# Attention and two MoE layers on one core: the second group's q loads move to ScalarE's queue, the third pair's v cast to GpSimd, and half of the x casts to ScalarE

## The chip, the cores and the metric

The kernel runs on one core of a Trainium2 chip. The core has a matrix engine (TensorE, PE in the profile; its weight loads are the row PEld), VectorE (DVE), ScalarE (ACT), GpSimd (POOL) and SyncE (SP), which only issues transfers here. The metric is device time in microseconds for one launch, the median of several runs.

## The reference, cut to what matters

```python
# attention: q, k, v are (2, 12, 448, 64), cap = 30
scores = q @ k.T / sqrt(64)
scores = cap * tanh(scores / cap)
attn = exp(scores) / sum(exp(scores))
x = (attn @ v), heads side by side: 896 tokens x 768
# first MoE layer: 768 -> 2048 -> 768
h = x @ w_in1
x = where(h > 0, h, exp(min(h, 0)) - 1) @ w_out1
# second MoE layer: 768 -> 2048 -> 768
h = maximum(x @ w_in2, 0)
out = (h * h) @ w_out2
```

The weights arrive as 64-bit floats. The kernel computes in pairs of 32-bit parts: each operand is split into a high part, rounded to the type that TensorE multiplies, and a low part, the rest; a product is high by high, high by low and low by high.

## The kernel before

**Tiling.** The 24 heads are taken as 12 pairs of heads, n = 0 to 11; two pairs (four heads) form a group, whose q, k and v are loaded together. A head's 448 rows are three full chunks of 128 and a tail of 64. The tails of k and q have their own tiles, `kz` and `qz`, those of v the tile `vs`.

**One pair** passes through these steps. `turn(n)` transposes its k and q chunks on TensorE into the PSUM tile `pt`. `high(n)` copies `pt` to the high part `kqh` on ScalarE and `low(n)` makes the low part `kql` on VectorE. `scores(n, c)` for c = 0 to 3 multiplies k by q into a PSUM tile `sc`, of which there are two, so each waits until the `tanh` two before it has read its tile. `tanh(n, c)` and `exp(n, i)` run on ScalarE and write the tile `e`. `split_p(n, i)` splits `e` into `ph` and `pl` on VectorE (i = 0 are the first four blocks, i = 1 the rest; both tiles exist once). `prep_v(n)` splits v into `vh` (cast) and `vl` (subtraction). `pv(n, i)` multiplies on TensorE into `po`. `pv_out(n)` copies `po` to `pvs` on ScalarE and moves the sums of exp to `den`. `norm(n)` takes their reciprocal `rd` on VectorE and sends it through DRAM (`far`, `bc`). `norm_x(n)` multiplies (`xn`) and splits the result into `xh` and `xl`, the operands of the first MoE layer.

**Order.** The whole program is written out by hand: every engine runs its instructions in the order of the code. The loop over n works on several pairs at once: in round n ScalarE and VectorE handle the scores of pair n, TensorE the products of pair n-1 and the transposes of pair n+2, and VectorE the normalisation of pair n-3. TensorE's order in a round is scores(n, 2), pv(n-1, 1), scores(n, 3), turn(n+2), scores(n+1, 0) and (n+1, 1), pv(n, 0). In round 0 nine idle products (18 matmul rows) stand where pv(n-1, 1) would be, and turn(2) comes behind scores(1, 1).

**Queues.** Nearly all transfers are issued on SP's queue, one after the other; at the start group 0's first q, `cap` and one piece of weights are on ScalarE's queue. Group 1 (pairs 2 and 3) is loaded while pair 0 is worked on. Each of SP's and ScalarE's transfers raises one of eight semaphores (DMAHW0 to DMAHW7), which are handed out in turn over both queues, and a transfer is issued only when the transfer before it on its semaphore has landed.

**Behind the loop** the MoE layers run on TensorE (`mm_in`, `moe1_out`, `moe2_out`), with the weights split piece by piece on VectorE and ScalarE while TensorE multiplies.

Of the kernel before, what the change touches and what calls it, by code (L numbers as in the profile page):

```python
# [26 lines left out]
def attention_moe_kernel(  # L27
# [12 lines left out]
    nc = tc.nc  # L40
    B, H, S, D = q.shape
# [46 lines left out]
    qzs = [one.tile([P, 4, D], F32, name=f"qz{i}") for i in range(2)]  # L88
# [4 lines left out]
    def fill_kq(i, eng):  # L93
        eng.memset(kzs[i], 0.0)
        eng.memset(qzs[i][D:], 0.0)
# [4 lines left out]
        if i < 2:  # L100
            eng.memset(vss[i][:, :, D:], 1.0)

    def load_group(g, what="kqvw", pp=None, dma=nc.sync.dma_start):

        if 2 * g >= len(pairs):
            return
        b, hp = pairs[2 * g]
        h0, nh = (0, 4) if pp is None else (2 * pp, 2)
        hs = slice(2 * hp + h0, 2 * hp + h0 + nh)
        if g not in nat:  # L110
            nat[g] = {x: lp.tile([P, NFULL, 4, D], F32, name=x, tag=x) for x in "kqv"}
        tail = slice(NFULL * P, S)
        for x, src in (("k", k), ("q", q)):
            if x in what:
                t = nat[g][x][:, :, h0:h0 + nh]
                src = src[b, hs]
                for c in range(NFULL):
                    dma(  # L118
                        t[:, c], src[:, c * P:(c + 1) * P].rearrange("h p d -> p h d")
                    )  # L120
                if x == "q":
                    dma(
                        qzs[g % 2][:D, h0:h0 + nh], src[:, tail].rearrange("h p d -> p h d")
                    )
                else:
                    for hh, r in enumerate(ROWS):
                        dma(
                            kzs[g % 2][r, h0 // 2:(h0 + nh) // 2, r],
                            src[hh::2, tail].rearrange("h p d -> p h d"),
                        )  # L130
        if "v" in what:
            for c in range(NFULL):
                dma(
                    nat[g]["v"][:, c, h0:h0 + nh],
                    v[b, hs, c * P:(c + 1) * P].rearrange("h p d -> p h d"),
                )
        if "w" in what:
            for hh, r in enumerate(ROWS):
                dma(
                    vss[g % 2][r, h0 // 2:(h0 + nh) // 2, :D],  # L140
                    v[b, hs][hh::2, tail].rearrange("h p d -> p h d"),
                )

    def prep_v(n):
        if n >= len(pairs):
            return
        g, pp = divmod(n, 2)
        vh, vl = vhs[n % 3], vls[n % 3]
        vn = nat[g]["v"][:, :, 2 * pp:2 * pp + 2]
        h, l = (t.rearrange("p (c h) d -> p c h d", h=2)[:, :, :, :D] for t in (vh, vl))  # L150


        (nc.vector if n > 1 else nc.gpsimd).tensor_copy(h, vn)
        nc.gpsimd.tensor_tensor(l, vn, h.bitcast(F32), op=ALU.subtract)


# [2 lines left out]
    def turn_one(to, n, u, c):  # L159
        g, pp = divmod(n, 2)  # L160
        hs = slice(2 * pp, 2 * pp + 2)
        if c < NFULL:
            src = nat[g]["kq"[u]][:, c, hs].rearrange("p h d -> p (h d)")
        elif u == 0:
            src = kzs[g % 2][:, pp]
        else:
            src = qzs[g % 2][:, hs].rearrange("p h d -> p (h d)")
        nc.tensor.transpose(to, src, ident)  # L168
# [25 lines left out]
    def idle_products(to, n):  # L194
        for _ in range(n):
            nc.tensor.matmul(to[:, 0, :P], ident, ident, start=True, stop=True)

    def first_pair():

        idle = psc.tile([P, 2, W], F32, name="sc", tag="sc")
        warm = lambda n: idle_products(idle, n)
        qk = [ap_.tile([P, 2, W], F32R, name=x, tag=x) for x in ("kqh", "kql")]
        st["qk", 0] = qk
        warm(8)
        pieces = []
        for u, cs, pool, tag, after in (
            (0, range(NFULL), ps1, "pt", 2),
            (1, range(NFULL + 1), ps1, "po", 0),  # L210
            (0, range(NFULL, NFULL + 1), psc, "sc", 6),
        ):
            t = pool.tile([P, 2, W], F32, name=tag, tag=tag)
            at = slice(cs[0] * P, (cs[-1] + 1) * P)
            for c in cs:
                turn_one(t[:, u, c * P:(c + 1) * P], 0, u, c)
            warm(after)
            pieces.append((t[:, u, at], *(x[:, u, at] for x in qk)))
        for t, h, l in pieces:
            nc.scalar.copy(h, t)  # L220
        for t, h, l in pieces:
            nc.vector.tensor_tensor(l, t, h.bitcast(F32), op=ALU.subtract)
# [27 lines left out]
    def exp(n, i):  # L250
        e = st["e", n][:, PARTS[i]]
        nc.scalar.activation(e, e, AF.Exp, scale=capt)  # L252

    def split_p(n, i, copy=nc.vector.tensor_copy):
        if n < 0:
            return
        if i == 0:
            st["p", n] = [
                ap_.tile([P, NB - 1, S], F32R, name=x, tag=x, bufs=1) for x in ("ph", "pl")
            ]  # L260
        blocks = slice(PARTS[i].start, min(PARTS[i].stop, NB - 1))
        e, h, l = (t[:, blocks] for t in [st["e", n]] + st["p", n])
        copy(h, e)
        nc.vector.tensor_tensor(l, e, h.bitcast(F32), op=ALU.subtract)
# [52 lines left out]
    def norm_x(n, copy=nc.vector.tensor_copy):  # L317

        if n < 0:
            return []  # L320
        b, hp = pairs[n]
        xn = ap_.tile([P, S], F32, name="xn", tag="xn")
        hi, lo = xh[:, hp, b * S:(b + 1) * S], xl[:, hp, b * S:(b + 1) * S]

        def x():
            for u, r in enumerate(ROWS):
                nc.vector.tensor_tensor(  # L327
                    xn[r], st["pvs", n][:D, u], st["bc", n][:, u], op=ALU.mult
                )

        return [
            x,
            lambda: copy(hi, xn),  # L333
            lambda: nc.vector.tensor_tensor(lo, xn, hi.bitcast(F32), op=ALU.subtract),  # L334
        ]
# [154 lines left out]
    def emit(steps):  # L490
        for step in steps:
            step()
# [42 lines left out]
    with tc.manual_schedule():  # L535
        fill_kq(0, nc.vector)
        load_group(0, "k", 0)
        load_group(0, "q", 0, dma=nc.scalar.dma_start)
        nc.scalar.dma_start(capt, cap.unsqueeze(0).to_broadcast([P, 1]))
        ws.load(nc.scalar.dma_start)  # L540
        load_group(0, "kq", 1)
        load_group(0, "vw", 0)
        fill_kq(1, nc.gpsimd)
        load_group(1, "kq")
        load_group(0, "vw", 1)
        ws.load()
        load_group(1, "vw")
# [2 lines left out]
        fill_v(2, nc.gpsimd)  # L550
        np_ = len(pairs)
        first_pair()
        nc.vector.reciprocal(tsc, capt)
        nc.vector.tensor_scalar(tsc, tsc, 1.0 / math.sqrt(D), None, op0=ALU.mult)
        prep_v(0)
# [18 lines left out]
        for n in range(np_):  # L574
            last = n == np_ - 1
            tanh(n, 0)
            if n:
                high(n + 1)
            tanh(n, 1)
            if not n:  # L580
                high(n + 1)
            split_p(n - 1, 1)
            prep_v(n + 1)
            exp(n, 0)
            low(n + 1)
            if n == 2:
                emit(second[3:])
            scores(n, 2)
            pv(n - 1, 1)
            scores(n, 3)  # L590
            if n:
                turn(n + 2)
            else:
                idle_products(ps1.tile([P, 2, W], F32, name="po", tag="po"), 9)
            norm(n - 2)
            if last:
                emit(ws.start())
            tanh(n, 2)
            pv_out(n - 1)
            if 2 <= n < 7:  # L600
                ws.load()
            tanh(n, 3)
            exp(n, 1)
            emit(norm_x(n - 3))
            split_p(n, 0)
            if n == 1:
                second = ws.whole()
                emit(second[:3])
            scores(n + 1, 0)
            scores(n + 1, 1)  # L610
            if not n:
                turn(2)
            if last:

                begun.append(new_acc())
                mm_in(0, 0, begun[0], xh, xl, kb[0:6:2])
            pv(n, 0)

            if n % 2:
                load_group((n + 3) // 2, "qv" if n > 1 else "v")  # L620
            else:
                load_group(n // 2 + 2, "k" if n else "kq")
                load_group(n // 2 + 1, "w" if n else "")


# [12 lines left out]
        x, x_high, x_low = norm_x(np_ - 2)  # L638
# [9 lines left out]
        x, x_high, x_low = norm_x(np_ - 1, nc.scalar.copy)  # L648
# [166 lines left out]
```

## Time and profile before

| | |
|---|---|
| median of 3 runs | 595.95 us (595.73 to 596.18) |
| the profiled execution | 594.1 us, span 592.3 us |
| PE busy in the span | 583.4 us (98%) |
| PEld, DVE, ACT, POOL busy | 89%, 72%, 56%, 5% |
| granted TensorE clock, mean | 0.997 |

The span runs from the first instruction to the last one of the profiled execution; 1.8 us of its time lie around it. Times within the span are given as us from its start. A row of the timeline gives start, duration, engine, line of the kernel, operation, tiles, count and, in brackets, the engine's idle time before it with what ended it.

### The profile page before, as it was taken

The page shows a single profiled execution, that of the slowest core. Times are in us where ns is not written, and L with a number is a line of the kernel's source. Part 1 is how long each engine was busy: PE and PEld are TensorE (multiplying, and loading weights), DVE is VectorE, ACT ScalarE, POOL GpSimd, SP SyncE. Part 2 cuts the span into 40 slices and gives each one's busy share as a digit, 9 for nine tenths or more (in the row PEclk, how much of TensorE's full clock was granted, in tenths as well). Part 3 has the DMA queues.
Part 4 walks back from the last instruction along what each step waited for, and adds up shares of the span by engine and source line. Part 5 has one row for each costly group of instructions (what it writes and reads, how often), then busy time and mean ns, then how long its engine had stood idle before and what let it go on. Part 6 is the DMA issues. An engine that isn't in the chain of part 4 may idle for free.

```text
span 592.3 us, 8596 instructions
## 1 busy us (share of the span) xinstructions
PE 583.4 (98%) x3062; PEld 528.0 (89%) x3062; DVE 425.0 (72%) x845; ACT 334.2 (56%) x484; POOL 32.1 (5%) x46
## 2 busy tenths in 40 slices
PE   8899999999999999999999999999999999999997
PEld 8677777788999999999999999999999999999997
DVE  4599999989999888665666657777777599981000
ACT  5699999827898777433333335666666645441000
POOL 3110110000000000000000000000000011230000
PEclk9899999999999999999999999999999999999999
DMA  5645651024444333233333344333333346622000
GB/s 128 158 103 140 161 148 42 33 75 144 135 133 134 106 98 100 76 128 106 116 98 107 111 132 132 107 107 107 108 114 113 108 136 184 184 70 106 24 23 37
DMA packets 81980, 64.76 MB, mean 109 GB/s; under 512 B 38416, under 2 KB 77072, under 8 KB 81936
## 3 DMA queue, kind: packets, MB, share of 16 engines
q1 hardware_dynamic: 80432, 63.58, 36.8%
q10 hardware_dynamic: 1504, 0.62, 0.4%
q8 instruction: 24, 0.39, 0.3%
q14 instruction: 20, 0.16, 0.1%
HBM read 61.34 MB, written 2.80 MB: 108 GB/s over the span
## 4 chain that ended last, share of the span: by engine, by line
PE 90%; DMA 3%; DVE 3%; SPq 2%; ACT 1%; issue 1%; POOL 0%; ACTq 0%; POOLq 0%; DVEq 0%
PE acc L522 19%; PE acc L523 19%; PE acc L521 19%; PE po L287 8%; PE acc L746 7%; PE acc L745 7%; PE acc L747 7%; PE sc L235 4%; PE pt L168 1%; DMA q<-in_q_dram 1%; SPq L118 1%; DVE xn L327 1%; DMA far<-rd 1%; DMA bc<-far 1%; DMA qz<-in_q_dram 0%
## 5 line engine op out<-in xcount | busy, mean ns | idle before, releaser
L521 PE MATMUL acc<-xh,wh 128*128 128x448 f32 x384 | 139.8, 364 | 1.2 <-ACT xh L333 1.2
L522 PE MATMUL acc<-xl,wh 128*128 128x448 f32 x384 | 140.0, 365 | 0.2 <-DVE xl L334 0.2
L523 PE MATMUL acc<-xh,wl 128*128 128x448 f32 x384 | 139.9, 364 | 0.0
L446 ACT CAST wh<-wf 128x384 fp32r<-128x384 f32 (+2 forms) x114 | 57.9, 508 | 107.2 <-PE acc L522 87.5
L391 ACT ACTIVATE wf<-wst 128x384 f32<-128x384 f32 (+2 forms) x130 | 70.5, 543 | 60.5 <-DVE wl L441 33.7
L441 DVE TENSOR_TENSOR wl<-wf,wh 128x384 fp32r<-128x384 f32 (+2 forms) x116 | 63.6, 548 | 55.9 <-ACT wh L446 55.8
L521 PEld LDWEIGHTS acc<-xh,wh 128*128 128x128 f32 x384 | 72.1, 188 | 7.1 <-ACT xh L333 1.5
L522 PEld LDWEIGHTS acc<-xl,wh 128*128 128x128 f32 x384 | 72.1, 188 | 5.9 <-DVE xl L334 0.5
L523 PEld LDWEIGHTS acc<-xh,wl 128*128 128x128 f32 x384 | 72.1, 188 | 5.7 <-DVE wl L441 0.3
L432 DVE SCALAR_TENSOR_TENSOR wf<-wst,wf 128x384 uint32<-128x384 uint32 (+3 forms) x132 | 71.1, 539 | 0.1
L425 DVE SCALAR_TENSOR_TENSOR wf<-wst,wf 128x384 uint32<-128x384 uint32 (+3 forms) x132 | 70.9, 537 | 0.0
L522 PE MATMUL acc<-gl,wh 128*128 128x448 f32 x192 | 70.0, 365 | 0.0
L523 PE MATMUL acc<-gh,wl 128*128 128x448 f32 x192 | 70.0, 364 | 0.0
L521 PE MATMUL acc<-gh,wh 128*128 128x448 f32 x192 | 69.8, 364 | 0.0
L404 DVE TENSOR_SCALAR wf<-wf 128x384 uint32<-128x384 uint32 (+3 forms) x132 | 54.4, 412 | 0.7
L400 DVE TENSOR_SCALAR wf<-wf 128x384 f32<-128x384 f32 (+3 forms) x132 | 45.7, 346 | 7.5 <-ACT wf L391 7.5
L244 ACT ACTIVATE e<-sc,tsc 128x896 f32<-128x896 f32 (+1 forms) x48 | 43.4, 911 | 2.9 <-PE sc L235 2.9
L732 DVE COPY o<-acc 128x432 f32<-128x432 f32 (+1 forms) x8 | 4.5, 557 | 53.8 <-PE acc L747 45.7
L746 PE MATMUL acc<-wl,gh 128*128 128x432 f32 x112 | 40.3, 359 | 0.0
L745 PE MATMUL acc<-wh,gh 128*128 128x432 f32 x112 | 40.0, 357 | 0.0
L747 PE MATMUL acc<-wh,gl 128*128 128x432 f32 x112 | 39.9, 356 | 0.0
L252 ACT ACTIVATE e<-e,capt 128x1792 f32<-128x1792 f32 (+1 forms) x24 | 38.6, 1609 | 0.8
(94 smaller groups left out, 933.0 us busy)
## 6 DMA issues: line engine op xcount, KB each, us to landing
wst<-in_moe_w_in_dram SPq DMA_DIRECT2D x63, 384.0 KB, 3.2
wst<-in_moe_w_out_dram SPq DMA_DIRECT2D x24, 384.0 KB, 3.2
wst<-in_moe_w_out_dram SPq DMA_DIRECT2D x16, 432.0 KB, 3.2
wst<-in_moe_w_out_dram SPq DMA_DIRECT2D x16, 336.0 KB, 2.9
wst<-in_moe_w_out_dram SPq DMA_DIRECT2D x12, 256.0 KB, 2.7
bc<-far SPq DMA_DIRECT2D x12, 224.0 KB, 3.3
k<-in_k_dram SPq DMA_DIRECT2D x15, 128.0 KB, 3.7
q<-in_q_dram SPq DMA_DIRECT2D x15, 128.0 KB, 2.9
```

Of the source, the lines that this page charges most:

```text
L391: nc.scalar.activation(self.f[i], hi.bitcast(F32), AF.Abs)
L404: v.tensor_scalar(fb, fb, 3, 0x3FFFFFFF, op0=ALU.logical_shift_left, op1=ALU.bitwise_and)
L425: v.scalar_tensor_tensor(out=fb, in0=hi, scalar=0xC0000000, in1=fb, op0=ALU.bitwise_and, op1=ALU.bitwise_or,)
L432: v.scalar_tensor_tensor(out=fb, in0=lo, scalar=29, in1=fb, op0=ALU.logical_shift_right, op1=ALU.bitwise_or,)
L441: (v if dst is None else nc.gpsimd).tensor_tensor(wl, self.f[i], wh.bitcast(F32), op=ALU.subtract)
L446: (v.tensor_copy if self.alone else nc.scalar.copy)(wh, self.f[i])
L521: nc.tensor.matmul(acc, w[0], x[0], start=first, stop=False)
L522: nc.tensor.matmul(acc, w[0], x[1], start=False, stop=False)
L523: nc.tensor.matmul(acc, w[1], x[0], start=False, stop=last)
L745: nc.tensor.matmul(acc, gh[:, f, gs], w[0], start=a, stop=False)
L746: nc.tensor.matmul(acc, gh[:, f, gs], w[1], start=False, stop=False)
L747: nc.tensor.matmul(acc, gl[:, f, gs], w[0], start=False, stop=z)
```

## The change

Four edits. (1) `load_group` gets a letter "z" for the tail of q, which was part of "q". Group 1's three q chunks are no longer issued on SP's queue between its k and its q tail, but on ScalarE's queue, at the place in the code behind `first_pair()`; the tail stays on SP's queue. (2) The cast of `vh` for pair 2 moves from VectorE to GpSimd. (3) In odd rounds (3, 5, 7, 9 and 11, pairs 0, 2, 4, 6 and 8) the cast of `xh` moves from VectorE to ScalarE, behind exp(n, 1). (4) In these rounds `xl` on VectorE moves behind split_p(n, 0).

```diff
-    def load_group(g, what="kqvw", pp=None, dma=nc.sync.dma_start):
+    def load_group(g, what="kqzvw", pp=None, dma=nc.sync.dma_start):
...
-                if x == "q":
-                    dma(
-                        qzs[g % 2][:D, h0:h0 + nh], src[:, tail].rearrange("h p d -> p h d")
-                    )
-                else:
+                if x == "k":
                     for hh, r in enumerate(ROWS):
...
+        if "z" in what:
+            dma(qzs[g % 2][:D, h0:h0 + nh], q[b, hs, tail].rearrange("h p d -> p h d"))
...
-        (nc.vector if n > 1 else nc.gpsimd).tensor_copy(h, vn)
+        (nc.vector if n > 2 else nc.gpsimd).tensor_copy(h, vn)
...
-        load_group(1, "kq")
+        load_group(1, "kz")
         load_group(0, "vw", 1)
         ws.load()
         load_group(1, "vw")
...
         first_pair()
+        load_group(1, "q", dma=nc.scalar.dma_start)
         nc.vector.reciprocal(tsc, capt)
...
-            emit(norm_x(n - 3))
-            split_p(n, 0)
+            if n % 2:
+
+                steps = norm_x(n - 3, nc.scalar.copy)
+                emit(steps[:1])
+                split_p(n, 0)
+                emit(steps[1:])
+            else:
+                emit(norm_x(n - 3))
+                split_p(n, 0)
```

The other calls of `load_group` with "q" get "qz" and load what they loaded.

**ScalarE at the start of the program.** Before, `kqh` of the first pair is followed by the first `tanh` (`e` from `sc`). In brackets stand the semaphores that an instruction waits for.

```order
L220 CAST kqh<-sc 128x128 [waits PE_49]
L244 ACTIVATE e<-sc,tsc 128x896 [waits DVE_49,PE_49]
L244 ACTIVATE e<-sc,tsc 128x896 [waits PE_49]
L186 CAST kqh<-pt 128x960 [waits PE_49]
L252 ACTIVATE e<-e,capt 128x1792 [waits DMAHW0_49,Activation_49]
```

And with the change:

```order
L218 CAST kqh<-sc 128x128 [waits PE_49]
L118 DMA q<-in_q_dram 128x4x64 [waits DMAHW0_49]
L118 DMA q<-in_q_dram 128x4x64 [waits DMAHW2_49]
L118 DMA q<-in_q_dram 128x4x64 [waits DMAHW5_49]
L242 ACTIVATE e<-sc,tsc 128x896 [waits DVE_49,PE_49]
L242 ACTIVATE e<-sc,tsc 128x896 [waits PE_49]
L184 CAST kqh<-pt 128x960 [waits PE_49]
```

The three loads of group 1's q now stand ahead of the first tanh, each with a wait for one of the eight transfer semaphores.

**SP's queue at the same time, with the change.** `vs_100` is group 0's v tail, `k` of 128x4x64, `kz_91` and `qz_93` are group 1's, the `v` behind them is group 0's second pair.

```order
L137 DMA vs_100<-in_v_dram 64x64 [waits DMAHW0_49]
L118 DMA k<-in_k_dram 128x4x64 [waits DMAHW1_49]
L118 DMA k<-in_k_dram 128x4x64 [waits DMAHW2_49]
L118 DMA k<-in_k_dram 128x4x64 [waits DMAHW3_49]
L123 DMA kz_91<-in_k_dram 64x2x64 [waits DMAHW4_49,Pool_49]
L123 DMA kz_91<-in_k_dram 64x2x64 [waits DMAHW5_49]
L128 DMA qz_93<-in_q_dram 64x4x64 [waits DMAHW6_49]
L131 DMA v<-in_v_dram 128x2x64 [waits DMAHW7_49]
L131 DMA v<-in_v_dram 128x2x64 [waits DMAHW1_49]
L131 DMA v<-in_v_dram 128x2x64 [waits DMAHW3_49]
L137 DMA vs_100<-in_v_dram 64x64 [waits DMAHW4_49]
L137 DMA vs_100<-in_v_dram 64x64 [waits DMAHW6_49]
```

Three `q` rows that stood ahead of `qz_93` are gone from here. Each transfer raises the semaphore that it waits for, in turn; numbers 0, 2 and 5 are skipped in the second turn (behind the row with DMAHW7), where ScalarE's three loads hold them.

**VectorE in round 3 (pair 0's x).** Before:

```order
L327 TENSOR_TENSOR xn<-pvs,bc 64x448 x2
L333 CAST xh<-xn 128x448
L334 TENSOR_TENSOR xl<-xn,xh 128x448
L263 CAST ph<-e 128x1792
L264 TENSOR_TENSOR pl<-e,ph 128x1792
L263 CAST ph<-e 128x896
```

With the change:

```order
L325 TENSOR_TENSOR xn<-pvs,bc 64x448 x2
L261 CAST ph<-e 128x1792
L262 TENSOR_TENSOR pl<-e,ph 128x1792
L332 TENSOR_TENSOR xl<-xn,xh 128x448
L261 CAST ph<-e 128x896
```

The cast `xh` is gone from VectorE, and `xl` stands behind `pl`.

## Rows read from the trace of the kernel before

**Rows 1.** The page: span, and busy time of each engine.

```profile
span 592.3 us, 8596 instructions
PE 583.4 (98%) x3062; PEld 528.0 (89%) x3062; DVE 425.0 (72%) x845; ACT 334.2 (56%) x484; POOL 32.1 (5%) x46
```

**Rows 2.** Windows of 1 us: length, then busy us of PE, PEld, DVE, ACT, POOL, clock, DMA.

```profile
21.00:22.00 1.00, 1.00 (x4) 0.87 (x4) 0.00 (x0) 1.00 (x2) 0.50 (x1) 0.50 0.20 48
```

**Rows 3.** Timeline, 16 to 33: turn(2), high(2), pair 2's vh, two pv.

```profile
17.12 0.14 PEld L168 LDWEIGHTS pt<-ident,kz 128*128 128x128 f32 x1 [0.29 <-DMA kz<-in_k_dram]
...
19.99 1.73 PE L287 MATMUL po<-ph,vh 128*128 128x448 f32 x4
...
20.21 0.96 ACT L186 CAST kqh<-pt 128x960 fp32r<-128x960 f32 x1 [2.32 <-PE pt L168]
...
24.16 0.47 PE L235 MATMUL sc<-kqh 64*128 64x448 f32 x2
...
26.01 0.55 DVE L153 CAST vh<-v 128x384 fp32r<-128x384 f32 x1 [7.04 <-DMA v<-in_v_dram]
...
27.68 0.31 PEld L168 LDWEIGHTS pt<-ident,k 128*128 128x128 f32 x3 [0.25 <-DVE kql L192]
...
30.11 1.09 PE L287 MATMUL po<-ph,vh 128*128 128x448 f32 x4
...
32.78 0.47 PE L235 MATMUL sc<-kqh 64*128 64x448 f32 x2
```

**Rows 4.** Timeline of ScalarE, 0 to 12 (ACTq: the transfers that it issues).

```profile
0.73 1.55 ACTq L118 DMA_DIRECT2D q<-in_q_dram  x3
...
4.25 1.28 ACT L220 ACT_TABLE_LOAD   x1 [4.25 <-DMA q<-in_q_dram]
...
7.68 0.27 ACT L220 CAST kqh<-sc 128x128 fp32r<-128x128 f32 x1
9.67 1.91 ACT L244 ACTIVATE e<-sc,tsc 128x896 f32<-128x896 f32 x2 [1.72 <-PE sc L235]
```

**Rows 5.** Timeline of SP's queue, 0 to 18: start, length of issuing, tiles, count.

```profile
10.64 1.12 SPq L139 DMA_DIRECT2D vs<-in_v_dram  x2
...
13.61 1.67 SPq L127 DMA_DIRECT2D kz<-in_k_dram  x2
...
17.06 0.61 SPq L122 DMA_DIRECT2D qz<-in_q_dram  x1
```

**Rows 6.** Waits of SP's queue, 0 to 20: total us, times, longest.

```profile
SPq L118 <- DMA q<-in_q_dram: 0.4, 1, 0.4
```

**Rows 7.** Timeline of TensorE, 0 to 17: idle products, scores and turn(2).

```profile
1.57 3.78 PE L196 MATMUL sc<-ident 128*128 128x128 f32 x16 [1.57 <-POOL ident masks.py:199]
...
11.20 0.47 PE L235 MATMUL sc<-kqh 64*128 64x448 f32 x2
...
12.72 2.17 PE L196 MATMUL po<-ident 128*128 128x128 f32 x18
15.06 0.47 PE L235 MATMUL sc<-kqh 64*128 64x448 f32 x2 [0.17 <-ACT e L244]
...
16.49 0.55 PE L168 MATMUL pt<-ident,k 128*128 128x128 f32 x3
```

**Rows 8.** Timeline, 47 to 72: TensorE waits for pl and for a q load.

```profile
49.02 0.71 PEld L287 LDWEIGHTS po<-pl,vh 128*128 128x128 f32 x4 [0.25 <-DVE pl L264]
...
71.80 0.14 PEld L168 LDWEIGHTS pt<-ident,q 128*128 128x128 f32 x1 [0.35 <-DMA q<-in_q_dram]
```

**Rows 9.** Waits, 72 to 105: total us, times, longest.

```profile
ACT pvs L296 <- PE po L287: 1.2, 3, 0.7
```

**Rows 10.** Chain that ended last, 103 to 140, where pair 8's x is made and behind.

```profile
114.02 0.40 DVE xh L333
114.45 0.63 DVE xl L334
...
134.00 0.57 ACT xh L333
```

More of the change, by code (lines that the diff above doesn't have):

```diff
@@ L113, in load_group @@
         for x, src in (("k", k), ("q", q)):
+            src = src[b, hs]
             if x in what:
                 t = nat[g][x][:, :, h0:h0 + nh]
-                src = src[b, hs]
                 for c in range(NFULL):
@@ L537, in attention_moe_kernel @@
         load_group(0, "k", 0)
-        load_group(0, "q", 0, dma=nc.scalar.dma_start)
+        load_group(0, "qz", 0, dma=nc.scalar.dma_start)
         nc.scalar.dma_start(capt, cap.unsqueeze(0).to_broadcast([P, 1]))
         ws.load(nc.scalar.dma_start)
-        load_group(0, "kq", 1)
+        load_group(0, "kqz", 1)
         load_group(0, "vw", 0)
         fill_kq(1, nc.gpsimd)
-        load_group(1, "kq")
+        load_group(1, "kz")
         load_group(0, "vw", 1)
@@ L619, in attention_moe_kernel @@
             if n % 2:
-                load_group((n + 3) // 2, "qv" if n > 1 else "v")
+                load_group((n + 3) // 2, "qzv" if n > 1 else "v")
             else:
-                load_group(n // 2 + 2, "k" if n else "kq")
+                load_group(n // 2 + 2, "k" if n else "kqz")
                 load_group(n // 2 + 1, "w" if n else "")
```

## The prediction

> **What bounds the kernel now.** I read the page first, then the windows of the first 32 us, then the timeline there engine by engine, then the rounds, then the end of the chain. TensorE is busy for 583.4 of 592.3 us [rows 1], so time can be won or lost only where TensorE waits or runs at its lower clock. Behind the loop it multiplies almost without a gap, so what shifts the loop shifts the end. In the loop a round is about 8.6 us, and TensorE, ScalarE and VectorE are all nearly full.
>
> The one large hole is at the start. turn(2), eight short transposes, begins at 16.49 [rows 7], waits 0.29 us for group 1's kz, then for its q and qz, and pv(0, 0) behind it starts only at 19.99. ScalarE, whose next work is high(2), idles 2.32 us until 20.21 [rows 3]. Then the granted clock is low: 0.50 in 21 to 22 (that is 1.2 of 2.4 GHz) [rows 2], and pv(0, 0) with the way to the next scores needs from 19.99 to 24.16, 4.17 us, where pv(1, 0) needs 2.67 (30.11 to 32.78) [rows 3].
>
> **Edit 1: q on ScalarE's queue.** On SP's queue it does what it looks like. The issuing of the three q fills the time from the end of kz (13.61 + 1.67) to qz at 17.06 [rows 5], so qz of group 1 moves up by 1.7 us. On ScalarE the three transfers stand between the last cast of `first_pair` (it ends at 7.95) and the first tanh (it starts at 9.67, after 1.72 us of idleness that scores(0, 1) ended) [rows 4]. At 0.52 us each (1.55 / 3) [rows 4] the issuing alone, 1.55 us, would lie within that idleness.
>
> But each of the three waits for a transfer semaphore. By the order of the built program these are numbers 0, 2 and 5, and the transfers before them on those three are SP's: the second vs of group 0, the second k of group 1 and the second kz of group 1. The first is issued at about 11.2 (10.64 and half of 1.12) and the last at about 14.4 (13.61 and half of 1.67) [rows 5], both long after 7.95. When the last lands can be read from TensorE: its transposes of kz start at 17.12, after a wait for just that [rows 3]. That such a wait holds the engine with all its later work shows twice in the trace. Before the table load at 4.25, which needs no data, ScalarE is idle for 4.25 us, put down to a q transfer [rows 4]: the weights' load ahead of it waits for an early q to land. And SP, whose fifth k waits for a q that ScalarE issued, loses 0.4 us to it [rows 6]: the waits reach across the queues.
>
> So ScalarE stands from 7.95 to about 17.12, issues the last q in 0.52 us and starts the first tanh at about 17.65 instead of 9.67: 8.0 us late. That removes the hole's cause (q lands in time) and puts a larger one ahead of it. Behind the held instruction are all of pair 0's tanh and exp, high(1), and through them scores(0, 2), scores(1, 0), split_p(0, 0) and pv(0, 0).
>
> How much of the 8.0 us arrives at the end? ScalarE's work from the first tanh to the end of tanh(1, 0) takes from 9.67 [rows 4] to 17.89 (20.21 - 2.32) [rows 3], 8.22 us, and the 2.32 us of idleness behind it absorb a part. TensorE's side decides:
> - Lower bound, TensorE at full clock: scores(1, 0) shift from 15.06 to 23.04 and turn(2) from 16.49 to 24.47 [rows 7]; nothing is missing there, so it lasts about 1.0 us (the next one, at 27.68, is followed by pv at 30.11 [rows 3], with 1.4 us of scores between, as from 15.06 to 16.49). pv(0, 0) starts at 25.5, lasts 2.67, and scores(1, 2) start at 28.2, against 24.16 [rows 3]: 4.0 us late.
> - Upper bound, with a long time at the half clock: TensorE now idles from about 11.2 + 0.1 (turn(1) is done, scores(0, 2) wait for the tanh) to 18.7, longer than the hole that cost it the clock in before. At the program's start an idle product took 0.24 us (3.78 / 16), in round 0 0.12 (2.17 / 18) [rows 7]. If the low clock holds until 23.5, as long as it held at the start, scores(0, 2) and (0, 3) last 2.5 instead of 1.5 us (11.20 to 12.72), and ten of the 18 idle products run at 0.22 to 0.24. They end at 24.5, scores(1, 0) and (1, 1) at 26.0, turn(2) at 27.0, and scores(1, 2) start at 29.7: 5.5 us late.
> I take the middle, **4.8 us**: the clock does fall (a smaller hole made it fall), but it need not stay down for all of that time: in before pv(0, 0) lost 1.5 us to it (4.17 - 2.67) and the products behind it nothing.
>
> The Trainium skill ("DMA: Bandwidth & Descriptors", section "Issuing engines are not separate DMA queues") says that issuing from several engines saves the sequencer's issue time and nothing else. By that sentence alone edit 1 would be a gain of SP's 1.7 us; it is the first rival below. The 0.4 us that SP lost to ScalarE's q in this trace is a cost that it does not mention. The skill's "PSUM — Partial Sum Buffer", section "Engine vs sequencer instructions", calls ScalarE's queue a strict FIFO; with that, the hold of 8 us follows, and the table load at 4.25 agrees.
>
> **Edit 2: pair 2's vh on GpSimd.** In before VectorE stood 7.04 us for v, until 26.01, with low(2) and split_p(1, 0) behind it; TensorE lost only 0.25 us to it, at turn(3), 27.68 [rows 3]. With ScalarE late, v has landed long before it is wanted, so the edit gives these **0.2 us** and no more. On GpSimd, which is 5% busy [rows 1], the cast costs nothing until pv(2, 0).
>
> **Edits 3 and 4: xh and xl in odd rounds.** VectorE loses 0.40 us of cast, and p is ready another 0.63 earlier [rows 10]. ScalarE gains a cast of 0.57 [rows 10] in five rounds, behind exp(n, 1); it waited 1.2 us in three rounds for po, 0.4 each [rows 9], so it falls behind by some 0.2 in an odd round and catches up in the even one. On TensorE the wait for pl goes (0.25 at 49.02), but the wait for group 4's q (0.35 at 71.80) [rows 8] depends on SP's chain of far, bc and den, which hardly moves, and keeps most of that. Gain **0.2**, between 0 and 0.6 (0.25 + 0.35). At the end the chain runs through VectorE's rows for pair 8's x (xh 0.40, xl 0.63) [rows 10]; xh leaves it and xl only changes its place: gain **0.4**, between 0 and 1.0 (xh and xl).
>
> **Sum.** 4.8 - 0.2 - 0.2 - 0.4 = 4.0 us more than the profiled 594.1, so 598.1 in a like execution. That execution lies 1.85 us below the median of 595.95, to which I add the same: **600.0 us**. Its own range: from 4.0 - 0.2 - 0.6 - 1.0 = +2.2 us to +5.5 us, so 598.2 to 601.5.
>
> **The rivals.**
> - *The waits are met early and only SP's 1.7 us counts (other side, faster).* It would need transfer semaphores that do not hold ScalarE at 7.95. Then qz lands 1.7 us earlier, the hole shrinks to about 0.5 us, and the clock stays up (1.5 us). With 3.2 at the start, 0.25 for turn(3), some 0.6 in the rounds and 0.4 at the end: -4.4 or -4.5, 591.5 us. For it: 1.72 us of idleness cover the issuing. Against it: the order of the program, and the two waits that hold a queue [rows 4, 6]. It decides if the first tanh starts at or before about 12. One in ten.
> - *ScalarE is held, but only to the first two of the three, or transfers land earlier.* If the kz that the last q waits for lands at 15 instead of 17.1, the first tanh is 2 us earlier and the loss about half: +2 or less, 597 to 598. Against it: TensorE itself waited for kz until 17.12. One in ten.
> - *The half clock lasts, or comes twice.* If pv(0, 0) too runs at half clock (another 1.5), or the q transfers, now in flight beside k and kz, delay the latter by half a microsecond, the loss is 6 to 7: 601.5 to 602.8. One in ten.
> - *ScalarE's hold is hidden: no change.* That takes 4 us of slack behind turn(2), and only 2.32 are in the trace. One in twenty.
>
> **How the numbers follow.** My forecast has 0.65, the rivals 0.10, 0.10, 0.10 and 0.05. A measurement of this kernel tells about 0.2% (1.2 us) from no change. Faster by more than that: the first rival, 0.10. Within: the last and a sliver of the second, 0.05. Slower: 0.85. The range 597.4 to 602.2 holds the forecast's own range, most of the second rival and half of the third: about eight in ten.
>
> **What the changed kernel's profile would show.** If I am right: three q transfers on ScalarE's queue spread from about 13 to 17.6 instead of lying side by side at 8 to 9.5; the first tanh near 17.6 with about 9 us of idleness put down to a transfer; TensorE idle from 11.3 to 18.7 and a clock of 0.5 behind it; no wait for q in turn(2); scores(1, 2) at 28 to 30; pv in the rounds with no wait for pl. I am wrong if the first tanh starts near 9.7, and the size is wrong if the clock stays at 1.0 through 20 (then the lower bound holds) or if the kz lands much later than 17.1.

## The result, and the profile after

The changed kernel takes **600.91 us** (median of 6 runs, 598.00 to 602.17) against 595.72 us of the kernel before beside it: ratio **1.0083**, 95% interval 1.0058 to 1.0108. It is slower by about 5 us. The forecast was 600.0 us. In a later comparison beside the kernel before (595.56 us) it took 599.90 us: 1.0065, from 1.0045 to 1.0085, so some 4 us. One execution of that comparison, the profiled one, ran at a granted clock of 0.75 and took 718 us; it is left out of the median, and its profile is not compared.

The page of its profiled execution (601.22 us), to be read beside [rows 1]:

```profile
span 599.4 us, 8592 instructions
...
PE 583.7 (97%) x3062; PEld 528.6 (88%) x3062; DVE 423.1 (71%) x839; ACT 336.3 (56%) x489; POOL 33.5 (6%) x47
```

TensorE is busy for 583.7 us, as before (583.4); the span is 7.1 us longer, so TensorE stands idle for 6.8 us more. The timeline of ScalarE at the start (columns as in [rows 4]) shows where:

```profile
6.77 0.59 ACT L218 CAST kqh<-po 128x512 fp32r<-128x512 f32 x1
7.25 0.28 ACT L218 CAST kqh<-sc 128x128 fp32r<-128x128 f32 x1
13.87 3.96 ACTq L118 DMA_DIRECT2D q<-in_q_dram  x3
17.93 1.91 ACT L242 ACTIVATE e<-sc,tsc 128x896 f32<-128x896 f32 x2 [10.40 <-DMA kz<-in_k_dram]
...
23.83 1.42 ACT L250 ACTIVATE e<-e,capt 128x1344 f32<-128x1344 f32 x1
26.34 1.01 ACT L242 ACTIVATE e<-sc,tsc 128x896 f32<-128x896 f32 x1 [1.09 <-PE sc L233]
```

ScalarE is done with `first_pair` at 7.53, issues the first of its three q at 13.87 and the last by 17.83, and starts the first tanh at 17.93 after 10.40 us of idleness that the landing of kz ended. Before, that tanh started at 9.67 [rows 4]: 8.26 us late. TensorE at the same time, to be read beside [rows 3, 7]:

```profile
11.15 0.33 PE L166 MATMUL pt<-ident,qz 128*128 128x128 f32 x1
18.99 0.74 PE L233 MATMUL sc<-kqh 64*128 64x448 f32 x2 [7.51 <-ACT e L242]
...
21.70 3.79 PE L194 MATMUL po<-ident 128*128 128x128 f32 x18
25.42 0.47 PE L233 MATMUL sc<-kqh 64*128 64x448 f32 x2
...
27.33 0.49 PE L166 MATMUL pt<-ident,q 128*128 128x128 f32 x3
27.66 0.27 PE L166 MATMUL pt<-ident,qz 128*128 128x128 f32 x1
27.69 1.06 PE L285 MATMUL po<-ph,vh 128*128 128x448 f32 x4
...
30.29 0.47 PE L233 MATMUL sc<-kqh 64*128 64x448 f32 x2
...
36.16 1.09 PE L285 MATMUL po<-ph,vh 128*128 128x448 f32 x4
```

turn(2) no longer waits for q or qz (27.33, 27.66), so the old hole is closed. In its place TensorE stands 7.51 us for the tanh, then runs slowly: the 18 rows of idle products take 3.79 us where they took 2.17 [rows 7]. scores(1, 2) start at 30.29 instead of 24.16, **6.13 us late**, and pv(1, 0) at 36.16 instead of 30.11 [rows 3]. The windows of 1 us (first the window, then busy times by engine, granted clock, share of the DMA engines, GB/s) show the clock:

```profile
14.00:15.00 1.00, 0.00 (x0) 0.00 (x0) 0.00 (x0) 0.00 (x0) 0.53 (x1) 0.93 0.97 220
15.00:16.00 1.00, 0.00 (x0) 0.00 (x0) 0.00 (x0) 0.00 (x0) 0.00 (x0) 0.50 0.98 220
...
24.00:25.00 1.00, 1.00 (x7) 1.00 (x6) 1.00 (x1) 1.00 (x1) 0.00 (x0) 0.50 0.87 193
25.00:26.00 1.00, 1.00 (x10) 0.85 (x11) 1.00 (x2) 0.25 (x1) 0.00 (x0) 0.95 0.36 73
```

It is 0.50 (1.2 of 2.4 GHz) in all ten windows from 15 to 25, though TensorE multiplies again from 18.99.

In the rounds the pv(n, 0) start at 36.16, 44.71, 53.26, 62.77, 71.26, 81.24, 89.73 and 98.28. Two steps are long: 9.51 us (53.26 to 62.77) and 9.98 us (71.26 to 81.24). Before, pv(8, 0) started at 90.80, so here it is 7.48 late: 1.4 us more than pv(1, 0). The waits of the weight loads and of VectorE (us in total, times, longest; 40 to 142 and 40 to 100) name three things that [rows 8] shows small or not at all:

```profile
PEld pt L166 <- DMA q<-in_q_dram: 1.8, 5, 0.5
```

```profile
DVE rd L307 <- DMA den<-pvs: 1.8, 3, 0.8
DVE xl L332 <- ACT xh L331: 0.9, 2, 0.5
```

TensorE waits for q, VectorE now waits for den in `norm`, and its xl waits for the xh that ScalarE now casts. At the end, the chain before has this row behind pair 8's x [rows 10]:

```profile
118.35 0.41 DVE wf L425
```

and with the change:

```profile
123.76 0.45 ACT xh L331
...
124.72 0.62 DVE xl L332
...
125.48 0.41 DVE wf L423
...
141.14 0.57 ACT xh L331
```

Behind pv(8, 0) some 0.4 us come back: pv(8, 0) is 7.48 late, `wf` behind pair 8's x 7.13 and the last xh 7.14 (before 134.00 [rows 10]). Pair 8's xh has not left the chain; it stands there on ScalarE. VectorE, from its first step on the weights in that round (112.08 before, 119.63 now) to rd (118.12, 125.25), needs 5.62 us instead of 6.04: about the 0.40 of its cast.

### The profile page after: what moved, and what is told of

It reads as the page before. It is cut to its first block, busy times and chain, and to the rows that moved or that the text cites. A ratio compares the mean times of both kernels' runs of the same rounds, so it can differ in the third digit from the quotient of the medians.

```text
span 599.4 us, 8592 instructions
## 1 busy us (share of the span) xinstructions
PE 583.7 (97%) x3062; PEld 528.6 (88%) x3062; DVE 423.1 (71%) x839; ACT 336.3 (56%) x489; POOL 33.5 (6%) x47
## 4 chain that ended last, share of the span: by engine, by line
PE 86%; DMA 4%; ACT 4%; DVE 2%; SPq 1%; issue 1%; POOL 0%; ACTq 0%; POOLq 0%
PE acc L520 19%; PE acc L521 19%; PE acc L519 19%; PE acc L752 7%; PE acc L751 7%; PE acc L753 7%; PE po L285 6%; PE sc L233 4%; ACT e L242 2%; DMA q<-in_q_dram 1%; ACT e L250 1%; PE pt L166 1%; DMA far<-rd 1%; DMA wst<-in_moe_w_in_dram 1%; DMA qz<-in_q_dram 1%
```

## The experiments

Each run's ratio is to the kernel before, run beside it. In the table stand the starts of the first tanh and of scores(1, 2), and the time from pv(1, 0) to pv(8, 0), all from the profiles: the first two price the start, the third the rounds (seven steps; at 8.55 us each 59.9).

| run | median us | ratio, 95% interval | tanh | scores(1, 2) | rounds |
|---|---|---|---|---|---|
| before | | | 9.67 | 24.16 | 60.69 |
| changed | 600.91 | 1.0083 (1.0058 to 1.0108) | 17.93 | 30.29 | 62.12 |
| e1 q on SP again | 595.29 | 0.9995 (0.9975 to 1.0015) | 9.69 | 24.53 | 61.97 |
| e2 edit 1 alone | 598.96 | 1.0045 (1.0025 to 1.0065) | 17.03 | 27.97 | 59.88 |
| e3 q on GpSimd | 592.39 | 0.9943 (0.9923 to 0.9963) | 9.36 | 21.57 | 62.00 |
| e4 one q on ScalarE | 596.64 | 1.0018 (0.9998 to 1.0037) | 13.68 | 24.93 | 62.01 |
| e5 changed, clock kept | 597.52 | 1.0033 (1.0017 to 1.0050) | 18.02 | 28.29 | 59.85 |
| e6 edits 3, 4 alone | 595.71 | 1.0004 (0.9984 to 1.0024) | 9.70 | 24.55 | 62.56 |
| e7 e3 and bc on GpSimd | 592.11 | 0.9944 (0.9928 to 0.9960) | 9.51 | 20.81 | 61.56 |
| e8 before, bc on GpSimd | 595.74 | 1.0007 (0.9990 to 1.0024) | 9.61 | 24.20 | 61.41 |
| e9 e3 and wst on GpSimd | 593.09 | 0.9966 (0.9940 to 0.9992) | 8.86 | 20.86 | 61.85 |
| e10 changed, wst on GpSimd | 599.32 | 1.0061 (1.0041 to 1.0082) | 17.31 | 28.59 | 61.05 |
| e11 changed again | 599.90 | 1.0065 (1.0045 to 1.0085) | | | |
| e12 e3 and v behind far | 592.67 | 0.9946 (0.9926 to 0.9965) | 9.70 | 20.76 | 62.33 |

### Which edit costs it

**e1**, edits 2 to 4 without edit 1:

```diff
-        load_group(1, "kz")
+        load_group(1, "kqz")
...
-        load_group(1, "q", dma=nc.scalar.dma_start)
```

> Edits 2 to 4 as in the change, but the q of the second group is issued by SP again. Theory (the hold of ScalarE by the three q transfers costs about 6 us, the other edits little): first tanh near 9.7, scores(1, 2) near 24.2, no idleness of 7 us on TensorE before it, and a time 0.2 to 1.5 us below the kernel before (ratio 0.9975 to 1.000). Rival A (edits 2 to 4 lose time by themselves, by ScalarE's extra cast or by SP's chain in rounds 4 and 6): first tanh near 9.7 as well, but 1 us or more above the kernel before (ratio over 1.0015), with the steps of rounds 4 and 6 near 9.5 and 10.0 us.

**e2**, edit 1 alone: `(nc.vector if n > 1 ...)` in `prep_v` and `emit(norm_x(n - 3)); split_p(n, 0)` as before.

> Edit 1 alone: the second group's q on ScalarE's queue; v's cast and the casts of x as in the kernel before. Theory (the hold costs it): first tanh near 17.9, scores(1, 2) near 30.3, and a time 5 to 7 us above the kernel before (ratio 1.008 to 1.012), with rounds 4 and 6 at their old 8.9 and 9.1 us if edits 3 and 4 made them longer, or near 9.5 and 10.0 if the later start does. Rival A (edits 2 to 4 carry a part of the loss): the same start, but 1.4 us or more less than the changed kernel. Rival B (the change of queue costs nothing): at most 1 us from the kernel before.

Without edit 1 the first tanh is back at 9.69 and the time at 0.9995: edits 2 to 4 cost or win nothing that can be told. Edit 1 alone costs 2.7 us (1.0045 of 596), and its rounds show no long step. That is less than the 5 to 7 us expected: in its profile the first tanh is 0.9 us earlier than in the changed kernel's, and the half clock ends at 21 to 22 instead of 25.

```profile
21.00:22.00 1.00, 1.00 (x9) 1.00 (x9) 0.50 (x1) 1.00 (x2) 0.27 (x1) 0.89 1.02 247
```

So scores(1, 2) are 3.8 us late there, not 6.1. The parts (2.7 and -0.3) do not add up to the 4 to 5 us of the whole; the intervals are 1.2 us to each side, so what is left, 1 to 3 us, is not settled.

### What holds ScalarE

**e4**: only the first of the three q on ScalarE, whose semaphore was last used by SP's second vs of group 0; the other two and qz on SP.

```diff
-    def load_group(g, what="kqzvw", pp=None, dma=nc.sync.dma_start):
+    def load_group(g, what="kqzvw", pp=None, dma=nc.sync.dma_start, chunks=range(NFULL)):
...
-                for c in range(NFULL):
+                for c in chunks:
...
-        load_group(1, "kz")
+        load_group(1, "k")
+        load_group(1, "qz", chunks=(1, 2))
...
-        load_group(1, "q", dma=nc.scalar.dma_start)
+        load_group(1, "q", dma=nc.scalar.dma_start, chunks=(0,))
```

> Edits 2 to 4, and only the first of the three q transfers of the second group on ScalarE's queue; the other two and qz on SP. Theory (ScalarE is held to the landing of the transfer before it on the same semaphore, here SP's second vs of the first group): the q on ScalarE is issued near 13.5, the first tanh starts near 14, 4 us later than before and 4 us earlier than in the changed kernel, and the time lies 1 to 4 us above the kernel before (ratio 1.0015 to 1.007). Rival D (ScalarE is held by anything common to all q transfers, such as the queue itself or the landing of kz): the first tanh near 17.9 as in the changed kernel, ratio over 1.008. Rival B (nothing holds it): first tanh near 9.7, ratio 1.000 or below.

ScalarE's timeline of this run:

```profile
13.19 0.37 ACTq L118 DMA_DIRECT2D q<-in_q_dram  x1
13.68 1.91 ACT L242 ACTIVATE e<-sc,tsc 128x896 f32<-128x896 f32 x2 [6.14 <-DMA vs<-in_v_dram]
```

How long ScalarE is held depends on what its q wait for: one q waits for vs and lets go at 13.56, three wait for kz and let go at 17.83. That is the theory's mechanism, at its place and time (expected near 13.5); rivals B and D fall. The ratio, 1.0018, is at the lower edge of what was expected, and its interval (0.9998 to 1.0037) does not tell it from no change.

**e3**: the same q, in flight as early, but issued by GpSimd.

```diff
         fill_v(2, nc.gpsimd)
+        load_group(1, "q", dma=nc.gpsimd.dma_start)
...
-        load_group(1, "q", dma=nc.scalar.dma_start)
```

> Edits 2 to 4, and the q of the second group issued on GpSimd's queue, behind the preparation of its first v buffers: still beside SP's transfers, but no compute engine of the start waits behind it. Theory (only the hold of ScalarE's in-order queue costs): first tanh near 9.7, turn(2) no longer waits for q, scores(1, 2) between 21 and 24, and a time 1 to 4.5 us below the kernel before (ratio 0.9925 to 0.998). Rival C (q in flight beside k and kz delays these, and that costs whoever issues it): kz lands later than 17.1, scores(1, 2) at 24.2 or later, a ratio of 1.000 or above.

GpSimd's row, then TensorE's of this run:

```profile
4.40 2.38 POOL L118 DMA_DIRECT2D q<-in_q_dram  x3
```

```profile
18.02 0.30 PE L166 MATMUL pt<-ident,kz 128*128 128x128 f32 x1 [0.83 <-DMA kz<-in_k_dram]
18.16 0.49 PE L166 MATMUL pt<-ident,q 128*128 128x128 f32 x3
18.82 0.30 PE L166 MATMUL pt<-ident,qz 128*128 128x128 f32 x1 [0.17 <-DMA qz<-in_q_dram]
18.94 1.05 PE L285 MATMUL po<-ph,vh 128*128 128x448 f32 x4
...
21.57 0.48 PE L233 MATMUL sc<-kqh 64*128 64x448 f32 x2
```

Here the waits of turn(2) for q are gone, pv(0, 0) runs at the full clock (2.63 us from 18.94 to 21.57, where it took 4.17 [rows 3]), and the kernel is 3.4 us **faster** than before. kz is waited for until 18.02, 0.9 later than in [rows 3]. That is not rival C's mechanism, though: in e7, e9 and e12, which start in the same way, the transposes of kz begin at 17.09 to 17.43, and in e6, with q on SP's queue, at 17.86. Where kz lands differs from execution to execution, and rival C's ratio of 1.000 or above did not come. The transfers of edit 1 were worth their move; the queue that they were moved to is what costs.

### How much of it is the clock

**e5**: the changed kernel with TensorE kept busy while it waits, by 31 idle products (62 of the matmul rows).

```diff
+            if not n:
+                idle_products(ps1.tile([P, 2, W], F32, name="po", tag="po"), 31)
             scores(n, 2)
```

> The changed kernel, with 31 idle products (7.2 us at 0.24 us each at the full clock) put on TensorE while it waits for the first tanh; they compute nothing that is used. It separates the clock from the lateness. Theory (about 2 of the 6.05 us by which pv(1, 0) is late come from the half clock behind the idle stretch, 4 from ScalarE's hold itself): the first tanh stays near 17.9, the granted clock stays at 1.00 from 10 to 28, the 18 idle products of round 0 take 2.2 instead of 3.8 us, scores(1, 2) start at 28.0 to 28.5 instead of 30.29, and the time is 1.5 to 2.5 us below the changed kernel (ratio to the kernel before 1.004 to 1.006). Rival (ScalarE's late chain alone sets the end of the start, the clock is hidden behind it): scores(1, 2) near 30 as in the changed kernel, ratio 1.008.

TensorE's timeline and a window of this run:

```profile
11.21 7.09 PE L194 MATMUL po<-ident 128*128 128x128 f32 x62
19.08 0.47 PE L233 MATMUL sc<-kqh 64*128 64x448 f32 x2 [0.78 <-ACT e L242]
...
20.69 2.17 PE L194 MATMUL po<-ident 128*128 128x128 f32 x18
...
28.29 0.47 PE L233 MATMUL sc<-kqh 64*128 64x448 f32 x2
```

```profile
20.00:21.00 1.00, 1.00 (x6) 0.95 (x7) 0.19 (x1) 1.00 (x2) 0.38 (x1) 1.00 0.30 50
```

The tanh is as late as in the changed kernel (18.02), the clock stays at 1.00, and scores(1, 2) start at 28.29. Of the 6.13 us, 4.13 are the hold and 2.00 (30.29 less 28.29) the clock. The ratio, 1.0033, lies below the 1.004 to 1.006 expected; in the profiled execution the rounds had no long step either.

The 2.00 belong to one execution. e10 (below) has the same program as the changed kernel until round 2, and TensorE's timeline there is

```profile
18.37 0.74 PE L233 MATMUL sc<-kqh 64*128 64x448 f32 x2 [7.44 <-ACT e L242]
...
21.07 2.72 PE L194 MATMUL po<-ident 128*128 128x128 f32 x18
...
28.59 0.47 PE L233 MATMUL sc<-kqh 64*128 64x448 f32 x2
```

After nearly the same wait (7.44 us) the full clock is back by 23, and scores(1, 2) are 4.43 late. From the first tanh to scores(1, 2) it is 10.27 us in e5, at the full clock, 10.94 in e2, 11.28 in e10 and 12.36 in the changed kernel: the half clock costs 0.7, 1.0 and 2.1 us.

### Where the rounds lose

**e6**, edits 3 and 4 alone in the kernel before:

> Edits 3 and 4 alone (who casts the high part of x, and when its low part is made), put into the kernel before. Theory (SP's chain of den, far and bc with its loads paces rounds 2 to 6, so that VectorE's 0.4 us in odd rounds win nothing there, and only the end of the chain wins some 0.3): 0 to 0.8 us below the kernel before (ratio 0.9985 to 1.000), with the waits of TensorE for q in rounds 4 and 6 together between 0.8 and 2.5 us, as often more as less than in the kernel before. Forecast of the prediction: 0.6 us below. Rival (edits 3 and 4 cost 1 us or more in the rounds): ratio over 1.0015.

1.0004, with TensorE's waits for q at 2.4 us (six times, to 0.8): neither the forecast's gain of 0.6 nor a loss of 1 us can be told from it. Its profiled execution (596.61 us, above the run's median) has the longest rounds of all, 62.56.

**e7 and e8**: bc issued by GpSimd in the loop, on e3 and on the kernel before.

```diff
-    def norm(n):
+    def norm(n, dma=nc.sync.dma_start):
...
-        nc.sync.dma_start(bc.rearrange("p h s -> p (h s)"), flat.to_broadcast([D, 2 * S]))
+        dma(bc.rearrange("p h s -> p (h s)"), flat.to_broadcast([D, 2 * S]))
...
-            norm(n - 2)
+            norm(n - 2, nc.gpsimd.dma_start)
```

> As the run with the second group's q on GpSimd's queue, and in the loop bc is issued by GpSimd too, so that SP no longer waits for far to land. Theory (SP's chain is what makes TensorE wait for q in rounds 4 and 6; in the run with q on GpSimd these steps were 10.09 and 8.86 us instead of 8.55): all steps of pv from round 2 to 8 at 8.5 to 8.6 us, no wait of TensorE for q, and 1.5 to 2.5 us less than that run: 590 to 591 us, ratio 0.990 to 0.992. Rival (the q waits come from the transfers or from GpSimd's own delay in issuing): waits stay or move to bc, ratio 0.994 or more.

> The kernel before, with only bc in the loop issued by GpSimd instead of SP; none of the change's edits. Theory (SP's chain costs the kernel before the 0.37 and 0.51 us by which its steps of rounds 4 and 6 exceed 8.55; VectorE, full at 8.66 us a round, then becomes the pace): 0 to 0.9 us below the kernel before, ratio 0.9985 to 1.000, no wait for q, rounds of 8.55 to 8.66 us. Rival (GpSimd issues bc later than SP, VectorE's product with bc waits): ratio above 1.000 with waits of VectorE for bc.

The waits for q do go, as the theory said, but the time does not: 592.11 us is e3's. In e7 VectorE waits instead (1.4 us once), for a bc that GpSimd issues at 36.19 and that its product with pvs gets only at 41.94; from issue to landing bc takes (KB, median us)

```profile
bc<-far POOLq DMA_DIRECT2D x10, 224.0 KB, 4.3
```

against 3.4 on SP in e3; in e8 it is 5.1, against 3.3 in the kernel before. In e8 the later rounds take 8.65 to 8.67 us each. VectorE is busy for 8.44 us of each, and TensorE waits for its pl in each (1.0 us in four), so VectorE is the likely next bound, as expected; no run shows that by itself.

**e9 and e10**: instead, the five loads of weights in rounds 2 to 6 on GpSimd's queue, on e3 and on the changed kernel; **e11**: the changed kernel beside them.

```diff
             if 2 <= n < 7:
-                ws.load()
+                ws.load(nc.gpsimd.dma_start)
```

> As the run with the second group's q on GpSimd's queue; besides, the five loads of weights in rounds 2 to 6 are issued by GpSimd, while den, far and bc stay on SP. SP has about 0.63 us a round less to issue. Theory (SP's chain is too long for a round, which is why TensorE waits for q in rounds 4 and 6; the weights are in no hurry, so GpSimd's later landing, 4.3 against 3.3 us for bc, harms nobody): all steps of pv near 8.55 us, no wait for q, 1 to 2.5 us less than with q alone on GpSimd: 590 to 591.3 us, ratio 0.990 to 0.9925. Rival (the long steps come from a late landing here and there, whatever SP has to issue): steps of 9 us and more stay, ratio 0.994.

> The changed kernel itself, with only the five loads of weights in rounds 2 to 6 moved from SP's to GpSimd's queue. Theory (1 to 2 of the changed kernel's loss come from TensorE's waits for q, made by SP's chain): first tanh and scores(1, 2) as in the changed kernel (17.9 and 28 to 30.3), no wait for q in the rounds, and 1 to 2 us below the changed kernel run beside it (ratio to the kernel before 1.004 to 1.007). Rival (the whole loss is that of the start): no difference from the changed kernel run beside it, below 0.6 us.

> The changed kernel once more, beside the other two and the kernel before on one chip, with a second profile. Theory (how long the half clock lasts and how often SP's chain makes TensorE wait for q differ from execution to execution; the hold does not): first tanh at 17 to 18, scores(1, 2) at 28 to 30.5, steps of rounds 4 and 6 anywhere from 8.5 to 10 us; ratio 1.006 to 1.009. Rival (both lengths belong to the kernel): scores(1, 2) at 30.3 and steps of 9.5 and 10.0 us again.

Again no gain: 0.9966 against e3's 0.9943, and 1.0061 against 1.0065 of the changed kernel beside it. e11's ratio lies in the range expected; whether its start and its long steps repeat cannot be read from it. SP's rows of e9 show why less issuing does not help:

```profile
50.98 0.50 SPq L309 DMA_DIRECT2D far<-rd  x1
54.92 0.45 SPq L312 DMA_DIRECT2D bc<-far  x1
...
61.36 0.55 SPq L309 DMA_DIRECT2D far<-rd  x1
63.11 0.47 SPq L312 DMA_DIRECT2D bc<-far  x1
```

SP comes to far earlier, but far lands no earlier: 3.94 us to bc here, 1.75 in the next round, 2.48 and 1.82 in e3. What was saved in issuing is waited out, and VectorE then stands for den (1.8 us). The theory that SP's issuing is too long for a round falls; the rival, a late landing, is what the rows show. The weights are still in flight beside far in e9, from another queue; whether they delay it was not tested.

**e12**: what far stands behind. In e3, the loads of v behind den.

```diff
             pv_out(n - 1)
+            if n > 2 and n % 2 == 0:
+                load_group(n // 2 + 1, "v")
...
-                load_group((n + 3) // 2, "qzv" if n > 1 else "v")
+                load_group((n + 3) // 2, "qz" if n > 1 else "v")
```

> As the run with the second group's q on GpSimd's queue; besides, in the even rounds from 4 on SP issues the three loads of v behind that round's far, bc and den instead of ahead of them. Everything is still issued by SP. Theory (far, 3.5 KB, lands late because its transfer stands behind the data of q and v: from far to bc SP took 2.3 to 2.8 us in the rounds that issue q and v, 1.7 to 1.8 in the others, and 3.9 where SP had less to issue): from far to bc 1.7 to 2.0 us in all rounds, steps of pv in rounds 4 and 6 near 8.55 us, no wait for q over 0.3 us, 0.5 to 2 us less than with q alone on GpSimd: 590.4 to 591.9 us, ratio 0.991 to 0.9935. Rival (far's landing has nothing to do with v): 2.3 us and more from far to bc in these rounds, and no gain: ratio 0.994 to 0.995.

```profile
49.90 0.61 SPq L309 DMA_DIRECT2D far<-rd  x1
52.63 0.45 SPq L312 DMA_DIRECT2D bc<-far  x1
...
85.62 0.48 SPq L309 DMA_DIRECT2D far<-rd  x1
87.29 0.45 SPq L312 DMA_DIRECT2D bc<-far  x1
```

With no v ahead of it far takes 2.73, 2.16 and 1.67 us to bc in rounds 4, 6 and 8, where it took 2.48, 2.61 and 2.31 in e3, and 2.81 once behind k and vs (42.97 to 45.78); VectorE now waits 1.65 us for v. The time is e3's (592.67). The theory asked for 1.7 to 2.0 in all rounds and for a gain, and neither came; that v has a part in the later rounds is not excluded. What makes far land in 1.7 us in some rounds and in 2.3 to 4.0 in others stays open.

## Why the prediction was right, and where it was not

**The hold of ScalarE: right, in mechanism and size.** The forecast had the first tanh at 17.65, 8.0 us late; it came at 17.93, 8.26 late. e4 shows that the landings of the earlier transfers on the same semaphores set it, e3 that the early transfer itself is a gain. The Trainium skill ("DMA: Bandwidth & Descriptors", section "Issuing engines are not separate DMA queues") says that issuing from several engines saves only the sequencer's time to issue. e3 fits that: SP issues qz at 16.34 instead of 17.06 [rows 5], and nothing at the start waits behind GpSimd's q. The sentence does not speak of an issue that waits for a semaphore, and most of the 10.40 us in the changed kernel are such waits, not issue time; there the measurement decides.

**The start's cost: the term of 4.8 us was too small for the profiled execution, 6.1 there, and near for e10, 4.4.** Its lower bound was met: 4.0 us with scores(1, 2) at 28.2, and e5 measured 4.13 and 28.29. What was mis-sized is the clock's part: taken at 0.8, bounded at 1.5 by a half clock until 23.5 and ten slow idle products; in the profiled execution it held until 25 and made all 18 slow, 2.0 us. In e10 and e2, with the clock back by 23 and 22, it cost 1.0 and 0.7. So the size differs from execution to execution, which would fit the wide scatter of the changed kernel's runs (598.0 to 602.2). The time of 23.5 had no good source: it was read from slow products at the program's start, where the windows from 1 to 8 record a granted clock of 1.00.

**Edit 2: the term of -0.2 is the late start's, not the edit's.** In the changed profile TensorE has no wait at turn(3), as forecast. But e2, which leaves this cast on VectorE, has none there either (31.26 to 32.49): with the start this late v has landed, and the wait is gone without the edit. In e1, with the start early again, the wait of 0.25 is gone too; there the edit may earn it.

**The rounds: the term of -0.2 had the wrong sign in this execution.** The waits for pl went, as forecast. In their place xl waits for ScalarE's xh (0.9 us in two rounds), which the forecast gave no price. And the wait for q, which was to keep most of its 0.35, grew: rounds 4 and 6 lost 1.5 us more than before (9.51 and 9.98 against 8.92 and 9.06). The step that failed is "depends on SP's chain of far, bc and den, which hardly moves": from far to bc SP took 1.7 to 2.8 us by the round in the kernel before already, and up to 3.3 (60.19 to 63.53) in the changed one, and den and q are issued behind it. The profiles lean against edits 3 and 4: in six that differ otherwise only outside these rounds (changed, e1, e3, e4, e5, e6) the rounds take 61.97 to 62.56 us five times and 59.85 once, and 60.69 and 59.88 without the edits (before, e2). But the medians of e1 and e6 show no effect beyond some 1.5 us either way, so a lasting loss is not shown; nor is a gain.

**The end: right in size.** -0.4 forecast, about -0.4 found, and VectorE's part is shorter by its cast, as forecast. That xh would leave the chain is not what came: it stands in it on ScalarE.

**The sum** was nearer than its terms, and that is in part luck: 598.1 was forecast for an execution like the profiled one, and 601.2 came (1.45 of it up to pv(1, 0), forecast 4.6 late and 6.05 in fact; 1.6 in the rounds); the 1.85 us added for the median were not needed, since the profiled run lies above its median here. The rival of the lasting half clock (601.5 to 602.8) describes the profiled run better than my own case, the median lies in mine. The first rival's time, 591.5 us, is near what e3 took with q on GpSimd, 592.4, a queue that the rival did not have.

## What to carry to other kernels

A load put on the queue of an engine that computes is priced by what its issue waits for: look up which transfer used its semaphore last, and when that lands; here three issues of 0.5 us held ScalarE for 8 us, and one held it for 4. Put such loads on a queue whose engine nothing near needs, as in e3, which beats both kernels by 3.4 and about 8 us. A hole on TensorE costs on top of the delay what the half clock behind it takes, 0.7 to 2.1 us here; keeping TensorE busy with products of no use gave that back in e5 (scores(1, 2) at 28.29 instead of 30.29).

## What the runs showed of the hardware that was not expected

- The half clock outlived the idle stretch: TensorE multiplied from 18.99, and the granted clock stayed at 0.50 until 25; in e10, with the same program there, it multiplied from 18.37 and had the full clock back by 23, in e2 from 18.09 and by 22.
- A small transfer (far, 3.5 KB) took 1.7 us from its issue to that of bc in some rounds and 3.9 to 4.0 in others; issuing less ahead of it on SP's queue (e9) made it no earlier.
- bc issued by GpSimd took longer to land than from SP: 4.3 against 3.4 us (e7, e3) and 5.1 against 3.3 (e8, before), medians.
